# Sink keys and values of the later blocks folded into the preceding block's rows, with the displaced keys fetched in the load queue

## The chip, the cores and the metric

The kernel runs on one core of one Trainium2 chip. The metric is the device time of one execution in microseconds (us); a comparison uses runs of both kernels on the same chip, taken in the same rounds. Where runs of one kernel spread, those over 1.5% above its fastest count as slow, and ratios use the others.

## The reference, cut to what matters

Attention with four sink keys and a window of 128, per head, then a normalised MLP with a residual. Four batches, 8 heads, 768 rows, head size 64, so the row of the model has 512 elements.

```python
is_sink   = pos[None, :] < 4
rel       = pos[:, None] - pos[None, :]
in_window = (rel >= 0) & (rel < 128)
scores    = where(is_sink | in_window, scale * q @ k.T, -1e9)
a         = exp(scores - max) ; a = a / (sum(a) + 1e-9)
x         = concat_heads(a @ v)                        # (4, 768, 512)
xn        = (x - mean) / sqrt(var + 1e-6) * g_ln
out       = x + relu(xn @ w1) @ w2                     # 512 -> 2048 -> 512
```

The kernel cuts the rows into 24 blocks of 128, six to a batch. A block's queries see their own block, the block before (only those keys that the window reaches), and the four sinks of the batch. A block in row 2 to 5 of its batch sees the sinks in neither of those two blocks, so they need work of their own.

## The kernel before: the parts that matter

Every piece of work is a task with estimated costs per engine. A planner builds the static order of each engine's queue from them, and each engine works through its queue in that order. The planner takes, again and again, the ready task that can start first; what it believes about a cost decides what stands ahead of what. Blocks are taken in groups of four: a group's 4 x 128 rows go through the first MLP layer (`ph`, 64 wide matmuls) and the second (`pc`, 64 wide matmuls), and the attention of later blocks is laid between these matmuls.

```python
# scores of a block: window keys, then sinks (rows 2 to 5)
nc.tensor.matmul(ps[:, h2, hh, kb, :], lhsT=qkT[t - kb][rows, 1, hp, :], rhs=qkT[t][rows, 0, hp, :], ...)
for h2 in range(2):
    for hp in range(4):                                       # pk: 8 narrow matmuls
        nc.tensor.matmul(P["pk", t][32 * hp:32 * hp + 32, h2, :], lhsT=ks_of[b][:, h2, hp, :],
                         rhs=qkT[t][:, 0, hp, :], ...)
# ... cut: exponential on ScalarE, mask on VectorE ...
# values, per half block: two sink matmuls into po, then 8 window matmuls
nc.tensor.matmul(po[...][:, :, h2, :], lhsT=ES[t][:, h2, :], rhs=vs_t[b][...], ...)
nc.tensor.matmul(po[:, hh, :], lhsT=ee[:, h % 2, hh // 2, kb, :], rhs=vn[:, t - kb, h, :], ...)
# ... cut: normalisation po -> xt, sum -> xc (centred), then the transposed copy of xc ...

# loads, all in GpSimd's queue, in program order
def load(fn, land, take=(), desc=1024):
    i = plan.add({"POOL": 0.88}, [], fn, (0,), take=take, land=land, after=last_load[0], desc=desc)
# q and k of blocks 8 on, and all xc of later groups, are transposed by DMAs in SyncE's queue
DTR = set(range(8, NT))
```

Names used below: `qkn` is q and k of a block as loaded, `vn` its values, `qkT` the transposed q and k (scores need it), `xc` the centred rows, `xnt` their transposed copy (the first MLP layer needs all four blocks of a group), `ot` an output row. "SPq" and "POOLq" in a profile are the queues of SyncE and GpSimd. Groups are counted from 0 in tables, so group 2 is the third group; it holds blocks 8 to 11. "Landing" is the time from the issue of a DMA to its completion.

The softmax here doesn't subtract the row's maximum and nothing guards it: scores larger than these inputs give would overflow.

## Time and profile before

| | before |
|---|---|
| time | 227.5 us median (226.96 to 227.76) |
| TensorE busy | 217.0 of 225.4 us |
| first matmul of the first MLP layer | 20.26 us |
| scores of block 8 | 59.69 us |
| q of block 13 issued by GpSimd | 63.95 us |
| `xc` of block 11 written | 83.11 us |
| third group's first MLP matmul | 95.74 us |
| last matmul ends | 221.3 us |

The prediction below shows the page, the stages and the chain. Three lines of the timelines of before are added here. The columns are start (us), duration (us), engine, line, operation, output <- input, count, and in brackets the idle time ahead with what ended it.

```profile
59.69 0.62 PE L406 MATMUL ps<-qkT 64*128 64x128 bf16 x16 [0.45 <-DMA qkT<-qkn]
```

```profile
63.95 0.92 POOL L267 DMA_DIRECT2D qkn<-in_q_dram  x1
```

```profile
83.11 0.35 DVE L529 TENSOR_SCALAR xc<-xt,sums 128x512 bf16<-128x512 bf16 x1
```

TensorE waited only 0.45 us for block 8; block 13's q was under way 25 us before its scores (88.64 us).

### The profile page before, as it was taken

What the parts mean: (1) busy time and instruction counts of PE and PEld (TensorE: products, weight loads), DVE (VectorE), ACT (ScalarE), POOL (GpSimd) and SP (SyncE); (2) the same over time, 40 slices, a digit from 0 to 9 for tenths busy, and PEclk for the clock granted to TensorE, in tenths of its full rate; (3) what the DMA queues carried; (4) which work ended last, traced back from release to release, by engine and by line L of the source; (5) the groups of instructions that cost most, each with busy time, mean ns of one, the idle gap of its engine ahead of it and who ended that gap; (6) DMA issues with size and microseconds to landing.
All of it is one profiled execution on the core that took longest, in us unless ns stands there. A gap on an engine that the chain in (4) does not pass through costs nothing.

```text
span 225.4 us, 4783 instructions
## 1 busy us (share of the span) xinstructions
PE 217.0 (96%) x1921; PEld 121.0 (54%) x1948; DVE 135.0 (60%) x398; ACT 104.0 (46%) x166; POOL 76.0 (34%) x92
## 2 busy tenths in 40 slices
PE   8999999999999999999999999999999999999992
PEld 7766787655455554455555544454555544444440
DVE  5777998779577988863756873654854712100121
ACT  2386788344367731167641258633077600376000
POOL 7994366691695242933088000100000010000000
PEclk9999999999999999999999999999999999999999
DMA  7999999999999999999989994203221021200111
GB/s 43 139 157 206 182 184 209 166 173 192 218 150 129 144 140 189 175 185 191 94 103 158 168 209 88 51 17 102 71 48 23 3 70 47 93 0 3 47 71 69
DMA packets 108709, 26.52 MB, mean 118 GB/s; under 512 B 101520, under 2 KB 105616, under 8 KB 108688
## 3 DMA queue, kind: packets, MB, share of 16 engines
q0 software_dynamic: 79104, 13.64, 81.7%
q1 hardware_dynamic: 29584, 12.59, 30.1%
q8 instruction: 15, 0.25, 0.4%
q14 instruction: 6, 0.05, 0.1%
HBM read 27.27 MB, written 6.29 MB: 149 GB/s over the span
## 4 chain that ended last, share of the span: by engine, by line
PE 81%; DMA 8%; POOL 5%; DVE 3%; issue 1%; ACT 0%; POOLq 0%; ACTq 0%
PE ph L603 34%; PE pc L634 34%; PE ps L406 5%; DMA w1s<-in_moe_w_ch_dram 4%; DMA qkT<-qkn 3%; PE po L501 2%; PE po L504 2%; POOL qkn L267 2%; POOL vn L275 2%; POOL qkn L272 2%; PE po L496 2%; PE pk L413 1%; PE pt L347 1%; DVE xt L517 1%; DVE w1s L299 1%
## 5 line engine op out<-in xcount | busy, mean ns | idle before, releaser
L603 PE MATMUL ph<-xnt,w1s 128*128 128x512 bf16 (+1 forms) x434 | 88.9, 348 | 1.0 <-DVE h L617 0.3
L634 PE MATMUL pc<-w2s,h 128*128 128x512 bf16 x371 | 87.0, 379 | 1.1 <-issue 0.5
L619 ACT ACTIVATE h<-ph 128x512 bf16<-128x512 f32 (+1 forms) x84 | 45.8, 546 | 53.8 <-PE ph L603 52.1
L603 PEld LDWEIGHTS <-w1s 128*128 128x128 bf16 x448 | 41.5, 98 | 35.4 <-ACT h L619 0.5
L634 PEld LDWEIGHTS <-h 128*128 128x128 bf16 x384 | 35.8, 98 | 39.1
L435 ACT ACTIVATE e<-ps 128x1024 bf16<-128x1024 f32 (+1 forms) x48 | 43.7, 951 | 12.5 <-PE ps L406 12.5
L646 DVE SCALAR_TENSOR_TENSOR ot<-pc,rsg,xt 128x512 f32<-128x512 f32 x24 | 17.9, 747 | 38.9 <-PE pc L634 38.9
L548 POOL TENSOR_TENSOR rsg<-ve,eps_half 128x4 f32<-128x4 f32 x6 | 6.2, 1028 | 82.0 <-DVE ve L546 82.0
L267 POOL DMA_DIRECT2D qkn<-in_q_dram x24 | 21.9, 910 | 14.9 <-DMA qkT<-qkn 13.1
L444 DVE TENSOR_TENSOR e<-e,mask_std 128x1024 bf16<-128x1024 bf16 x28 | 18.9, 684 | 10.9 <-ACT e L435 10.9
L617 DVE TENSOR_SCALAR h<-ph 128x512 bf16<-128x512 f32 (+1 forms) x28 | 15.9, 570 | 13.7 <-PE ph L603 13.6
L272 POOL DMA_DIRECT2D qkn<-in_k_dram x24 | 21.7, 903 | 2.8 <-DMA w2s<-in_moe_w_ch_dram 1.4
L275 POOL DMA_DIRECT2D vn<-in_v_dram x24 | 21.8, 912 | 1.8 <-DMA w1s<-in_moe_w_ch_dram 1.8
L517 DVE SCALAR_TENSOR_TENSOR xt<-po,rc 128x256 bf16<-128x256 f32 x48 | 20.4, 425 | 1.7
L501 PE MATMUL po<-vn,e 128*128 128x65 bf16 x192 | 17.1, 193 | 0.1
L537 DVE BATCH_NORM_STATS2 st<-xt 128x6 f32<-128x512 bf16 x24 | 16.4, 684 | 0.0
L406 PEld LDWEIGHTS <-qkT 64*128 64x128 bf16 x352 | 9.9, 94 | 10.4 <-issue 7.8
L406 PE MATMUL ps<-qkT 64*128 64x128 bf16 x352 | 14.7, 218 | 0.7 <-DMA qkT<-qkn 0.4
L482 ACT ACTIVATE es<-pk 128x256 bf16<-128x256 f32 x16 | 6.1, 383 | 19.9 <-PE pk L413 19.8
L514 DVE RECIPROCAL rc<-po 128x4 f32<-128x4 f32 x48 | 8.5, 178 | 11.3 <-PE po L504 10.4
L501 PEld LDWEIGHTS <-e 128*128 128x128 bf16 x192 | 14.0, 97 | 2.1 <-DVE e L444 0.5
L504 PE MATMUL po<-vn,e 128*128 128x65 bf16 x160 | 14.9, 193 | 0.0
(66 smaller groups left out, 146.2 us busy)
## 6 DMA issues: line engine op xcount, KB each, us to landing
out_dram<-ot SPq DMA_DIRECT2D x24, 256.0 KB, 2.5
qkn<-in_q_dram POOLq DMA_DIRECT2D x24, 128.0 KB, 7.1
qkn<-in_k_dram POOLq DMA_DIRECT2D x24, 128.0 KB, 6.8
vn<-in_v_dram POOLq DMA_DIRECT2D x24, 128.0 KB, 7.6
w1s<-in_moe_w_ch_dram POOLq DMA_DIRECT2D x4, 512.0 KB, 10.3
w2s<-in_moe_w_ch_dram POOLq DMA_DIRECT2D x4, 512.0 KB, 10.7
qkT<-qkn SPq DMA_TRANSPOSE x16, 7.2
xnt<-xc SPq DMA_TRANSPOSE x16, 5.6
```

The lines of the kernel that those rows point to most:

```text
L267: nc.gpsimd.dma_start(qn[t][:, 0], q[b, :, rows, :].rearrange("h p d -> p h d"))
L272: nc.gpsimd.dma_start(qn[t][:, 1], k[b, :, rows, :].rearrange("h p d -> p h d"))
L275: nc.gpsimd.dma_start(vn[:, t, :, 0:64], v[b, :, rows, :].rearrange("h p d -> p h d"))
L406: nc.tensor.matmul(ps[:, h2, hh, kb, :], lhsT=qkT[t - kb][rows, 1, hp, :], rhs=qkT[t][rows, 0, hp, :], start=(hh == 0 and kb == 0 and t no ...
L435: nc.scalar.activation(E[t, half][:, :, :, 0:nkb, :], P["ps", t, half][:, :, :, 0:nkb, :], AF.Exp, scale=scale)
L444: nc.vector.tensor_mul(ee[:, :, 0:w], ee[:, :, 0:w], m[:, 0:w].unsqueeze(1).to_broadcast([128, 4, w]))
L501: nc.tensor.matmul(po[:, hh, :], lhsT=ee[:, h % 2, hh // 2, 0, :], rhs=vn[:, t, h, :], start=(r < 2 and hh == 0), stop=(r == 0), skip_grou ...
L504: nc.tensor.matmul(po[:, hh, :], lhsT=ee[:, h % 2, hh // 2, 1, :], rhs=vn[:, t - 1, h, :], start=False, stop=True, skip_group_check=True)
L517: nc.vector.scalar_tensor_tensor(xt[t][:, 256 * half:256 * half + 256].rearrange("p (h d) -> p h d", h=4), in0=po[:, :, 0:64], scalar=1.0, ...
L603: nc.tensor.matmul(ph, lhsT=w1s[:, j, 128 * ht:128 * (ht + 1)], rhs=xnt[g][:, j, cols], start=(j == 0), stop=(j == NDM - 1))
L619: nc.scalar.activation(o, i, AF.Relu)
L634: nc.tensor.matmul(P["pc", t], lhsT=h1[g, ht][:, 128 * ti:128 * (ti + 1)], rhs=w2s[:, ht, :], start=(ht == 0), stop=(ht == NH1 - 1))
```

## The change

The first four keys of the preceding block are almost useless to a later block: key 0 is outside the window of all its queries, and keys 1 to 3 are seen only by queries 0 to 2. So in blocks 14 to 17 and 20 to 23 the batch's sink keys and values are written over rows 0 to 3 of the preceding block's, after that block has used them. The window matmuls then do the sinks' work as well, and the eight sink matmuls for scores and four for values of each such block disappear. What queries 0 to 2 lose is computed apart: their rows of q, and the three displaced keys and values, are fetched in a row layout, worked out on VectorE in fp32 for all blocks at once ("the corrections"), spread by three DMAs (`fcb`), and added into `po` before the normalisation.

Besides, the planner gets other lags and start times for the opening, and may put a block's variance on ScalarE.

```diff
+    FOLD = 12
+    FETCH = 13
+        fold = r >= 2 and t >= FOLD
+            def fold_k(e): nc.vector.tensor_copy(qkT[t - 1][:, 1, :, 0:4], kss_of[b])
+            def fold_v(e): nc.vector.tensor_copy(vn[0:4, t - 1], vn[0:4, t - r])
-            sink = r >= 2 and halves[-1] == 1
+            sink = r >= 2 and not fold and halves[-1] == 1
...
+    def fetch(i, b):                              # row i of batch b: three small loads
+        def f(e):
+            nc.gpsimd.dma_start(fq[at], q[b, :, 256:768, :]...[i])
+            for to, src in ((fk, k), (fv, v)):
+                nc.gpsimd.dma_start(to[at]..., src[b, :, 129:641, :]...[:, :, 0:3, :]...)
+        fetched.append(load(f, .35, desc=96 * 3, cost=1.2))
...
+    def corrections():
+        def step(cost, deps, fn, eng="DVE"):
+            return plan.add({eng: cost}, deps, fn, (0, 7, 8))
+        # 3 products with q, 3 sums, exp, mask, 3 products with v, 1 sum, 2 additions
+        # then fcb[i:i + 1] <- fc[12 * i:12 * i + 12] for i in 0..2, on SyncE
...
+                if fold:
+                    nc.vector.tensor_add(po[0:3], po[0:3], fcb[:, t - RB - 2 * b, 4 * half:4 * half + 4, :])
...
+        if t == FETCH:                            # in the load queue ahead of block 13
+            for b in range(1, B):
+                for i in range(3):
+                    fetch(i, b)
         load_block(t)
```

(Cut: the new lags of loads and filler of the opening, the model of two DMA queues in the planner, smaller rings, and the ScalarE form of the variance.)

## The prediction

> **What bounds the kernel now.** I read the page first (busy shares, then the 40 slices), then the busy time by stages, the chain that ended last, and last the groups by shape.
>
> ```profile
> PE 217.0 (96%) x1921; PEld 121.0 (54%) x1948; DVE 135.0 (60%) x398; ACT 104.0 (46%) x166; POOL 76.0 (34%) x92
> ...
> PE   8999999999999999999999999999999999999992
> ```
>
> TensorE is busy 217.0 of 225.4 us; no other engine passes 60%. Only the first and the last slices fall off. By stages (us; busy time and count of PE, PEld, DVE, ACT, POOL; clock; DMA; GB/s):
>
> ```profile
> 20.00:26.50 6.50, 5.91 (x71) 4.51 (x69) 6.13 (x23) 5.13 (x11) 2.51 (x3) 1.00 1.40 199
> ...
> 60.50:79.10 18.60, 18.39 (x197) 10.13 (x198) 14.84 (x42) 13.85 (x22) 11.93 (x14) 1.00 2.03 157
> 79.10:95.80 16.70, 16.49 (x134) 8.41 (x135) 14.00 (x45) 3.86 (x5) 9.04 (x11) 1.00 1.77 168
> ...
> 179.80:221.30 41.50, 41.25 (x189) 18.58 (x190) 5.84 (x11) 10.15 (x17) 1.01 (x1) 1.00 0.14 48
> ```
>
> From 26.5 us on, TensorE is the bound in every stage. A microsecond of matmuls removed there is a microsecond off the end, unless a new wait appears. DVE has its least room from 79 to 96 us: 14.00 of 16.70 us. Up to about 20 us the loads set the time and TensorE is kept busy with filler matmuls. The chain that ended last, in order of time (start, us, what), shows what is to be removed:
>
> ```profile
> 105.20 0.62 PE ps L406 x16
> 105.82 0.23 PE pk L413 x8
> 106.05 2.70 PE ph L603 x12
> 108.74 0.12 PE po L496 x2
> ```
>
> Each block with a sink pays 0.23 us for eight narrow score matmuls (pk), and, for each half, 0.12 us for two sink matmuls into po. In the same chain 16 window-score matmuls take 0.55 us, and 49 wide ones 10.74 us, or 0.216 to 0.219 us each.
>
> [...] So the durations by group (220 to 380 ns) are latencies, and counts must be multiplied by steps. [...] q loads show 0.91 us on GpSimd and 7.1 us to landing. [...]
>
> **The change, part by part.**
>
> Removed on TensorE: eight blocks (14 to 17, 20 to 23) lose their sink matmuls, 8 x (0.23 + 2 x 0.12) = 3.8 us. Batches 2 and 3 lose two spreading matmuls each (pv), 4 x 0.11 = 0.44 us. **4.2 us**, all in the PE-bound part.
>
> Moved on TensorE: I compared the static order of the two builds. One half-block of attention (0.36) and one block's transposes (0.22) now stand ahead of the first MLP matmul, where the first w1 chunk (landing about 20 us) sets the time, and three filler matmuls after it are gone (0.15). That is 0.7 us more. Multiplying the two instruction lists from that matmul on by the steps above gives 196.0 us before and 191.1 after: **4.9 us**. In the trace the same stretch takes 201.0 us (20.3 to 221.3), so 5.0 us of small waits come on top, 1.5 of them before 26.5 us while DVE scales w1 between the last normalisations. I expect 0.3 of these to go, as the rescaled filler lets the early blocks finish sooner. Fillers ahead of 20 us cost nothing. The tail (last output row, store) is the same.
>
> DVE: added are 16 three-row additions in PSUM (0.41 each by the planner's own cost: 6.6 us), eight pairs of row copies (0.56 a pair: 4.5) and the corrections, 11 operations of 512 fp32 elements and four small ones, 11 x 0.69 + 0.8 = 8.4 us. Removed are four vs products (424 ns) and four ks copies (320), 3.0 us, and 13 of 24 variances (684 + 182 ns, 11.3 us), which go to ACT in the new order. With four more wide relus (0.69 each) the sum is about +8 us, 143 of 222. No bound on average. ACT gets 13 variances of about 1 us each (estimate from its 128x512 passes at 597 ns plus the small scaling) and loses eight exponentials (383 ns), four relus and a few copies: 104 to about 110. No bound.
>
> GpSimd and loads: 27 small loads enter the queue ahead of block 13. The one-core trace gives two sizes: 1024-descriptor loads start 0.87 apart, the four w1 loads of 512 descriptors (15.23 - 12.25)/4 = 0.745 apart. A straight line through these puts 32 descriptors at 0.62 us, so 27 take 16.9 us; the planner allows 0.4 each, 10.8 us.
>
> ```profile
> 58.56 1.03 POOL L548 TENSOR_TENSOR rsg<-ve,eps_half 128x4 f32<-128x4 f32 x1 [7.20 <-DVE ve L546]
> 59.56 0.93 POOL L272 DMA_DIRECT2D qkn<-in_k_dram  x1
> ...
> 84.39 0.74 DVE L646 SCALAR_TENSOR_TENSOR ot<-pc,rsg,xt 128x512 f32<-128x512 f32 x1
> 85.05 0.17 DVE L514 RECIPROCAL rc<-po 128x4 f32<-128x4 f32 x1
> ```
>
> Here GpSimd sits in order behind the power of group 1. In the new order that power follows block 3's output row, which ended just after 59.9 us; so the power ends near 62, block 12's k and v near 63.5, and the fetches start then. At 0.4 each they are issued by 74.3[...]; at 0.62 by 80.3[...]. The first correction stands in DVE's queue just after the first normalisation of block 11. In the new PE order block 11 comes earlier than the 85 us above: 54.8 us of work after the first MLP matmul, with 3.2 us of waits, or 78.3 on TensorE and 79.3 on DVE. **So at 0.4 us per fetch nothing waits, and at 0.62 DVE stands still about 3 us.** DVE is in order, so block 12's masks, block 11's centring and the output rows queue behind. TensorE has 44 wide matmuls (9.5 us) queued that need little of DVE, and the corrections take 8.4 us of that. A stall of 3 us on DVE therefore passes about 2 us on to TensorE, at block 12's AV near 91 or at the third group's first MLP matmul near 95. Block 13 itself, loaded at 80 to 82 in this case, transposed by 87 or 88, meets a need at 89.
>
> The row copies wait for the previous block's scores and AV, some 8 us earlier; I charge nothing.
>
> **The sum.** 4.9 + 0.3 = 5.2 us if the fetches are cheap, less about 0.3 for crowding on DVE: 227.5 - 4.9 = 222.6. At 0.62 us per fetch: 5.2 - 2.3 = 2.9, or 224.6. I weigh the first slightly more, for the planner's other costs (0.9 a load) match the trace: **223.3 us**.
>
> **Rivals.** (1) *The load queue becomes the wait.* If each fetch takes what a full load takes, 0.87 us, they end at 87,[...] DVE stops for 10 us and block 13 comes 5 us late: some 7 us lost, 229. For it: GpSimd's time depends little on the count of descriptors (0.745 against 0.87 for half). Against: it does depend. (2) *DVE becomes the bound around 79 to 96 us.* It had 14.0 of 16.7 us there; 8.4 us of corrections do not fit unless the variances leave it (they do, four or five of them, 4 us) and some work moves later. Block 11's centring is delayed behind them, and its transposed copy is needed by the third group. That alone would cost 1 to 3 us: 223.5 to 225.5. (3) *The removed work is all there is,* and earlier progress is lost again, because block 8's transposed q and k set the time at 59.7 us (TensorE waited 0.45 us there): then only 4.2 us, 223.3. (4) *The opening gains more than I charge:* all 1.5 us of waits before 26.5 go: 221.5.
>
> **Range and chances.** The 2% line is 222.94 us. Cheap fetches and an orderly DVE fall just below it, everything else above. I give 45% to fetches near 0.4 us (mostly below the line), 40% to some 0.6 (mostly above), 15% to dearer ones. That makes 0.41 for faster, 0.56 for within 2%, and 0.03 for slower, which would take 232 us. Range 221.0 to 226.8.
>
> **What would show it right or wrong.** In the profile after: pk 64 and po<-vs 32 instead of 128 and 64, PE busy down by 4 to 5 us. The spacing of the fetches on GpSimd is the number to look for: 0.4 or 0.6. The first correction's product on DVE should show idle time released by a DMA only in the latter case, and TensorE then a gap between 88 and 97 us. From 110 to 180 us each half of a group should be shorter by what the sinks cost, with TensorE at 98% as before. I am wrong if the gap on TensorE comes without a wait for the fetches (DVE crowding, or the transposes), if the additions to po hold PSUM banks so long that the stages after 110 us do not shorten, or if the start of the first MLP matmul moves from 20.3 us.

Cut from it, where marked, are rules that no trace of this case shows, and the landing time of a small load that was taken from one of them. The forecast of 223.3 us, between 222.6 (0.4 us a fetch) and 224.6 (0.62), was summed with that landing time, so terms of it are cut: it is a part of the 3 us for which VectorE was to stand still, of the 2.3 us taken off for them, and of the 10 us of rival (1). The numbers that stay have the fetches issued by 74.3 or 80.3 us against a first correction at 79.3; the rest of the 3 us was an assumption that no trace had shown. The steps by which the counts are multiplied can be read from the chain of before: 0.216 to 0.219 us for a wide matmul, 0.06 us for one into `po` of 130 columns (two in 0.12 us at 108.74), 0.055 us for one of 128 columns (four transposes in 0.22 us at 45.26). For the 0.69 us of a 512-element fp32 operation on VectorE that trace has only near ones: the statistics pass at 684 ns, the relu at 685 ns.

## The result, and the profile after

The changed kernel takes **238.31 us** (median of four runs, 236.60 to 239.85) against 227.52 us (226.96 to 227.76). The ratio is 1.0476, 95% interval 1.0388 to 1.0564: slower. A ratio here is the mean time of one kernel's fast runs over the mean of the other's of the same rounds, so it is not quite the ratio of the medians. Predicted were 223.3 us and a range to 226.8.

The page of after: busy times, TensorE in 40 slices, and the granted clock in the same slices (before, every slice of the clock was 9). The granted clock is the share of TensorE's full clock that the profile records.

```profile
PE 215.3 (92%) x1813; PEld 118.7 (51%) x1836; DVE 142.1 (61%) x420; ACT 109.6 (47%) x190; POOL 92.2 (39%) x120
...
PE   8799999999799994496999999999999999999993
...
PEclk9999999999999999587999999999999999999999
```

A slice is 5.87 us. The loss lies in three of the four slices from 88 to 111 us (4, 4, 9, 6); the clock is down in the last three of these (5, 8, 7). By stage, after and then before (same columns as in the prediction):

```profile
79.10:95.80 16.70, 11.37 (x76) 5.50 (x74) 10.77 (x25) 2.63 (x6) 16.61 (x23) 0.97 1.15 91
95.80:112.00 16.20, 11.92 (x85) 5.98 (x87) 8.57 (x31) 7.36 (x14) 7.71 (x9) 0.71 1.99 171
```

```profile
95.80:112.00 16.20, 15.95 (x147) 8.31 (x149) 9.46 (x26) 10.40 (x16) 3.73 (x5) 1.00 1.96 164
```

TensorE fell from 16.49 and 15.95 us to 11.37 and 11.92 us of work, and in the second stage that work ran at a mean clock of 0.71. GpSimd, by contrast, has not a free moment from 79 to 96 us: 16.61 of 16.70. VectorE is *less* busy than before, 10.77 against 14.00: it is not overloaded, it waits.

When the stages begin shows where the 9.6 us come from by which the last matmul of the profiled run ends later (start of each layer's first matmul, us):

| | before | after | difference |
|---|---|---|---|
| layer 1, group 1 | 60.47 | 61.19 | +0.72 |
| layer 2, group 1 | 79.09 | 80.17 | +1.08 |
| layer 1, group 2 | 95.74 | 107.57 | +11.83 |
| layer 2, group 2 | 112.75 | 125.28 | +12.53 |
| layer 2, group 3 | 145.63 | 157.03 | +11.40 |
| layer 2, group 4 | 179.66 | 189.23 | +9.57 |
| last matmul ends | 221.26 | 230.84 | +9.58 |

From 125 us on the changed kernel *regains* 3.0 us, which is the folding at work. Some 10.75 us are lost in one stage. The waits of TensorE around it:

```profile
60.41 0.62 PE L484 MATMUL ps<-qkT 64*128 64x128 bf16 x16 [1.76 <-DMA qkT<-qkn]
...
97.08 1.03 PE L484 MATMUL ps<-qkT 64*128 64x128 bf16 x16 [6.45 <-DMA qkT<-qkn]
...
107.57 1.02 PE L714 MATMUL ph<-xnt,w1s 128*128 128x512 bf16 x4 [2.15 <-DMA xnt<-xc]
```

Block 13's scores wait 6.45 us for its transposed q and k; ten microseconds later the third group's MLP waits for block 11's transposed copy. The chain that ended last (start, us, what; the pieces over these 60 us) runs through the second of these, not the first:

```profile
51.06 9.31 DMA qkT<-qkn
60.90 0.88 POOL qkn L295
...
63.71 8.84 DMA vn<-in_v_dram
73.42 5.02 DMA fv<-in_v_dram
84.56 2.28 DMA fv<-in_v_dram
98.63 8.81 DMA xnt<-xc
107.57 1.02 PE ph L714 x4
```

Each step can be seen in the queue of its engine. GpSimd first:

```profile
64.58 0.64 POOL L365 DMA_DIRECT2D fq<-in_q_dram  x1
...
70.84 0.59 POOL L365 DMA_DIRECT2D fq<-in_q_dram  x1 [2.71 <-DMA qkn<-in_k_dram]
72.84 0.59 POOL L367 DMA_DIRECT2D fk<-in_k_dram  x1 [1.41 <-DMA vn<-in_v_dram]
...
84.56 0.59 POOL L367 DMA_DIRECT2D fv<-in_v_dram  x1
85.14 0.95 POOL L295 DMA_DIRECT2D qkn<-in_q_dram  x1
```

The fetches start 0.58 to 0.61 us apart: 27 of them take some 15.8 us. Besides, three of them wait, 4.8 us in all, for a load issued earlier to land; each time it is the load eight places before in this queue (the seventh fetch waits for block 12's k, with block 12's v and six fetches between). Block 12's k and v took 7.8 and 8.8 us to land and so hold the fetch up. The instructions in the trace show where the eight comes from: the loads of this queue use eight completion semaphores in turn (numbers 99 to 106), and a load first waits on the one that it is to use (96 of the 99 loads after the first eight), that is for the landing of the load that had it last. So this wait is built into the program (kernel.py itself names no semaphore), and one slow load stops the queue eight loads later. Block 13's q is issued at 85.14, 21.2 us later than before. Then VectorE:

```profile
80.94 0.15 DVE L376 TENSOR_SCALAR mask_c<-iota_c 36x3 f32<-36x3 int32 x1
86.82 0.68 DVE L383 TENSOR_TENSOR fk<-fk,fq 36x512 f32<-36x512 f32 x1 [5.72 <-DMA fv<-in_v_dram]
...
96.17 0.35 DVE L634 TENSOR_SCALAR xc<-xt,sums 128x512 bf16<-128x512 bf16 x1
```

The planner believed in 0.4 us a fetch and placed the corrections where they would then have been ready. VectorE stands 5.72 us at the first of them, and block 11's `xc` comes behind the last, at 96.17 instead of 83.11. (The name in brackets is the profile's guess. The product waits for all eight semaphores; the last one to be reached was that of the last k fetch, issued at 83.98 and landed at 86.79. The last fetch of all, of v, issued at 84.56, landed at 87.72.) Last SyncE's queue:

```profile
96.03 2.49 SPq L397 DMA_DIRECT2D fcb<-fc  x3
98.63 1.42 SPq L676 DMA_TRANSPOSE xnt<-xc  x1
```

The three DMAs of the corrections go out just ahead of block 11's transposing DMA, which then takes 8.81 us to land, while the loads of blocks 13 on are being caught up. Which of the two makes that landing long is not separated by any run.

So there are **two ways** from the late fetch to TensorE: (a) block 13's own loads, (b) VectorE's wait, the corrections, block 11's `xc` and its transposed copy. The first hypothesis on this trace was that (a) with the lowered clock behind it is the loss; the chain favours (b). The experiments decide.

### The profile page after: what moved, and what is told of

Same layout as the page of the kernel before. It is cut to its first block, busy times and chain, and to the rows that moved or that the text cites. A ratio compares the mean times of both kernels' runs of the same rounds, so it can differ in the third digit from the quotient of the medians.

```text
span 234.8 us, 4652 instructions
## 1 busy us (share of the span) xinstructions
PE 215.3 (92%) x1813; PEld 118.7 (51%) x1836; DVE 142.1 (61%) x420; ACT 109.6 (47%) x190; POOL 92.2 (39%) x120
## 4 chain that ended last, share of the span: by engine, by line
PE 69%; DMA 16%; POOL 5%; DVE 5%; issue 2%; ACT 1%; SPq 1%; POOLq 0%; DVEq 0%
PE ph L714 30%; PE pc L745 27%; DMA qkT<-qkn 4%; PE ps L484 4%; DMA vn<-in_v_dram 4%; DMA xnt<-xc 4%; DMA fv<-in_v_dram 3%; DMA qkn<-in_q_dram 2%; PE po L601 2%; PE po L604 1%; PE pt L425 1%; POOL fk L367 1%; PE ps L475 1%; DVE ot L757 1%; DVE fk L383 1%
## 5 line engine op out<-in xcount | busy, mean ns | idle before, releaser
L730 ACT ACTIVATE h<-ph 128x512 bf16<-128x512 f32 (+1 forms) x79 | 43.0, 546 | 42.9 <-PE ph L714 42.3
L745 PEld LDWEIGHTS <-h 128*128 128x128 bf16 x384 | 36.3, 99 | 41.1 <-issue 1.8
L728 DVE TENSOR_SCALAR h<-ph 128x512 bf16<-128x512 f32 (+1 forms) x33 | 19.0, 581 | 12.5 <-PE ph L714 12.4
L484 PE MATMUL ps<-qkT 64*128 64x128 bf16 x352 | 15.5, 226 | 8.2 <-DMA qkT<-qkn 8.2
L484 PEld LDWEIGHTS <-qkT 64*128 64x128 bf16 x352 | 10.5, 98 | 17.9 <-DMA qkT<-qkn 8.9
L533 DVE TENSOR_TENSOR e<-e,mask_one 128x1024 bf16<-128x1024 bf16 x22 | 14.6, 686 | 4.4 <-ACT e L524 4.4
L601 PEld LDWEIGHTS <-e 128*128 128x128 bf16 x192 | 14.2, 99 | 4.5 <-DVE e L533 0.6
L604 PEld LDWEIGHTS <-e 128*128 128x128 bf16 x160 | 11.1, 97 | 2.2
L648 ACT ACTIVATE nb<-sums 128x1 f32<-128x1 f32 x13 | 2.6, 201 | 17.6 <-DVE sums L631 17.6
## 6 DMA issues: line engine op xcount, KB each, us to landing
w2s<-in_moe_w_ch_dram POOLq DMA_DIRECT2D x4, 512.0 KB, 10.9
```

The lines of the kernel that those rows point to most:

```text
L601: nc.tensor.matmul(po[:, hh, :], lhsT=ee[:, h % 2, hh // 2, 0, :], rhs=vn[:, t, h, :], start=(not sinks and hh == 0), stop=(r == 0), skip_ ...
L604: nc.tensor.matmul(po[:, hh, :], lhsT=ee[:, h % 2, hh // 2, 1, :], rhs=vn[:, t - 1, h, :], start=False, stop=True, skip_group_check=True)
L730: nc.scalar.activation(o, i, AF.Relu)
L745: nc.tensor.matmul(P["pc", t], lhsT=h1[g, ht][:, 128 * ti:128 * (ti + 1)], rhs=w2s[:, ht, :], start=(ht == 0), stop=(ht == NH1 - 1))
```

## The experiments

In every case the edit is on the changed kernel unless another is named. The kernel before took 227.5 to 228.0 us (medians). Runs named "wrong on purpose" leave up to three query rows of eight blocks uncorrected; that stays within the tolerance of the comparison.

### Take away the fetch, the corrections, or both

```diff
 # no fetch (wrong on purpose): three memsets on GpSimd in place of the 27 loads
-            nc.gpsimd.dma_start(fq[at], ...)       # and fk, fv
+            if (i, b) == (0, 1): nc.gpsimd.memset(fq, 0.0); nc.gpsimd.memset(fk, 0.0); nc.gpsimd.memset(fv, 0.0)
 # no corrections (wrong on purpose): planned as before, nothing emitted; zeros added into po
-            return plan.add({eng: cost}, deps, fn, (0, 7, 8))
+            return plan.add({eng: cost}, deps, lambda e: None, (0, 7, 8))
```

> The changed kernel with the 27 fetches of displaced rows not issued; three memsets on GpSimd stand in for them, so the corrections run on zeros (wrong result on purpose), everything else in the same order. Theory A (the fetches in the load queue make block 13's load and DVE's corrections late): the idle time of 6.5 us before block 13's scores, the wait of 5.7 us on DVE and the lower clock from 96 to 112 us all go; about 224 us. Rival B (the 8 us of corrections crowd DVE whatever the fetch does): 229 to 233, with TensorE still waiting for block 11's transposed copy. Rival C (the folding itself, or the planner's other changes): 234 or more.

> The changed kernel with all 27 fetches, but without the corrections on DVE and ACT and without the spreading DMAs; the additions to po add zeros (result wrong in the first three rows of eight blocks on purpose). Theory A in its first half (the load of block 13 comes late because it stands behind the fetches): TensorE still idles some 5 to 6 us before block 13's scores and the clock still falls; 231 to 235 us. Theory A in its second half (DVE waits for the fetch, and all that stands behind it is late) or rival B: the time falls to 224 to 227. Rival C: no change, 237.

> The changed kernel without fetches and without corrections (wrong result on purpose in the first three rows of eight blocks): the folding of the sinks alone, in the same order of instructions. Theory A and rival B: about 223 to 224 us, since 3.8 + 0.44 us of matmuls are gone from the bound stages and block 8 sets the time at 60 us as before. Rival C in its first half (folding brings its own waits): 230 or more.

| | median us | ratio to before | 95% interval |
|---|---|---|---|
| fetch and corrections (the change) | 238.31 | 1.0476 | 1.0388 to 1.0564 |
| corrections alone (no fetch; one run of four slow) | 229.35 | 1.0026 | 0.9961 to 1.0092 |
| fetch alone (no corrections) | 235.92 | 1.0328 | 1.0277 to 1.0378 |
| neither (one run of four slow) | 225.16 | 0.9866 | 0.9829 to 0.9902 |

Without either, the folding is worth 1.3%: the saving of the prediction is real, though smaller than predicted. The fetch in its place costs most (10.8 us without corrections), the corrections without it 4.2 by the medians. Not all of the 4.2 is theirs: in the profiled executions the run without the fetch is 6.0 us behind the one with neither at the last matmul, and 3.0 of these it had lost by 82 us, ahead of the first correction, where block 8's scores waited 2.00 us instead of 0.99 and the clock behind it was lower (0.64 from 60.6 to 62 us, 0.50 to 64, 0.90 to 66). TensorE's waits, first without the fetch, then without the corrections:

```profile
101.23 1.18 PE L713 MATMUL ph<-xnt,w1s 128*128 128x512 bf16 x4 [2.75 <-DMA xnt<-xc]
```

```profile
98.42 1.04 PE L483 MATMUL ps<-qkT 64*128 64x128 bf16 x16 [7.10 <-DMA qkT<-qkn]
```

Each takes one way away and leaves the other: without the fetch block 13 is in time and only `xnt` is late; without the corrections `xnt` is in time and block 13 is as late as ever. Taking (b) away wins only 2.4 us of the 13, because (a) then sets the time. The lowered clock is on the path in that run: it was 0.50 from 94.3 to 104.6 us, so after the wait of 7.10 us the 6.1 us from 98.4 on lose (1 - 0.50) x 6.1 = 3.1 us more, 10.2 of the 10.8 together (an estimate).

### The planner's other changes alone

```diff
-    FOLD = 12
+    FOLD = 99          # no block folds; no fetch, no corrections
```

> The changed kernel with no block folded, no fetches, no corrections: only the planner's other changes (costs, filler, variance on ACT, smaller rings) over the kernel before; correct result. Theory A: 226.5 to 228.5 us, neutral. Rival C in its second half (the other changes cost the time): 232 or more. If the other changes had given something, 225 or less.

229.81 us, ratio 1.0051 (1.0001 to 1.0101; one run of four slow). The rest of the change is worth nothing or a little less than nothing. Block 8's scores waited 2.54 us in its profiled execution, the slow one. The waits at block 8 return below.

### Keep TensorE's clock up: filler matmuls in the wait

```diff
+                    if t == 13 and half == halves[0]:
+                        for _ in range(110):                # 6.3 us ahead of block 13's scores
+                            nc.tensor.matmul(ps..., lhsT=ident, rhs=ident, ...)
```

> The changed kernel with 110 filler matmuls (some 6 us) put ahead of block 13's scores, where TensorE stood idle 6.5 us. If the lower clock after that idle time costs by itself (in the trace 1.5 us at 0.50, 6.1 us at 0.74 and 4.5 us at 0.62, some 4 us of work lost), the clock stays up to block 13's successors and the time falls by 2 to 4 us, to 233 to 235. If only the idle time counts, no change or slightly slower: 237 to 239.

239.75 us, ratio 1.0504 (1.0437 to 1.0571): no gain, although the mean clock from 95.8 to 112 us rose from 0.71 to 0.92.

```profile
98.82 0.62 PE L488 MATMUL ps<-qkT 64*128 64x128 bf16 x16 [1.72 <-DMA qkT<-qkn]
...
109.96 1.87 PE L718 MATMUL ph<-xnt,w1s 128*128 128x512 bf16 x4 [4.99 <-DMA xnt<-xc]
```

What the clock gave back before 105 us was spent waiting for `xnt`. So the low clock between 97.1 and 101.7 us was *not on the path* of the change; (b) was. (The comparison is not exact: in this execution VectorE waited 6.60 us for the fetch instead of 5.72, and block 11's `xc` came 1.2 us later.) My expectation of the clock as part of the loss was wrong.

### A smaller fetch: batches 2 and 3 only

```diff
-            for b in range(1, B):        # 27 loads, corrections on 36 rows
+            for b in range(2, B):        # 18 loads, corrections on 24 rows
```

> The changed kernel with fetches and corrections for batches 2 and 3 only: no block of batch 1 is folded, so nine of the 27 fetches are never used. Correct result. 9 x 0.585 = 5.3 us less in the load queue. Theory A: the idle time before block 13's scores falls from 6.5 to about 1.2 us, DVE's wait from 5.7 to about 0.4, and the clock dips less: 228 to 231 us. If the loss came from the corrections on DVE instead (unchanged here, 36 or 24 partitions take the same time): 235 or more.

234.38 us, ratio 1.0298 (1.0253 to 1.0342).

```profile
92.38 0.62 PE L484 MATMUL ps<-qkT 64*128 64x128 bf16 x16 [0.54 <-DMA qkT<-qkn]
...
105.65 1.87 PE L714 MATMUL ph<-xnt,w1s 128*128 128x512 bf16 x4 [5.27 <-DMA xnt<-xc]
```

Way (a) is open here (0.54 us) and the time is still 3% above before: way (b) alone. VectorE waited 3.67 us for the fetch, and here that also reached TensorE directly: at 88.84 it waited 2.17 us for a mask that stands behind the first corrections. The 512-element operations of the corrections took 0.67 to 0.68 us on 24 rows here, as on 36 rows in the change. I had expected 228 to 231, having seen only (a).

### Leave all the work and tell the planner what it costs

```diff
-        fetched.append(load(f, .35, desc=96 * 3, cost=1.2))    # three loads
+        fetched.append(load(f, .35, desc=96 * 3, cost=2.1))
```

> The changed kernel with the planner told 2.1 us for each set of three fetches instead of 1.2 (the trace has 20.6 us for the 27, with waits), so that the static order fits. Theory: most of the loss came from an order that was planned with a wrong cost; MLP matmuls of the third group move ahead of block 13 and the corrections behind work that is ready: 226 to 230 us, DVE's wait for the fetch under 1 us. Rival: the load queue itself is late and every later block with it, whatever the order: 233 or more.

229.35 us, ratio 1.0037 (0.9972 to 1.0101; one run slow). The same 27 loads and corrections, ordered for 0.7 us a load, give back some 9 us. The wait was not gone, as I had expected (under 1 us): in the profiled execution VectorE still stood 4.25 us for the fetch, whose loads waited 7.1 us for others instead of 4.8. The profiled execution (231.82 us, the slow one) still had three waits on TensorE:

```profile
61.92 0.62 PE L484 MATMUL ps<-qkT 64*128 64x128 bf16 x16 [2.33 <-DMA qkT<-qkn]
...
95.33 5.30 PE L745 MATMUL pc<-w2s,h 128*128 128x512 bf16 x16 [2.08 <-DVE ot L757]
...
102.64 0.56 PE L484 MATMUL ps<-qkT 64*128 64x128 bf16 x14 [2.01 <-DMA qkT<-qkn]
```

### The smaller fetch with the corrections placed later

Edit: the fetch of batches 2 and 3, and priority (0, 13, 8) for the corrections instead of (0, 7, 8). Block 11's `xc` and its transposing DMA then stand ahead of most corrections and of `fcb`.

> The fetch of batches 2 and 3 alone (18 small loads in GpSimd's queue), with the corrections placed later in DVE's order, so that most of them and their three DMAs come after block 11's centring and its transposing DMA. Theory of two gates (block 13's late load, and DVE and SyncE held up ahead of block 11's centring and its transposed copy): both are open, waits at block 13 below 1 us and at the third group's first MLP matmul below 1.5 us, that matmul at 96 to 98.5 us, and a time of 227 to 230. Rival (late loads by themselves slow whatever follows: the transposing DMA lands late because the loads catch up): that matmul still waits 3 us or more, and the time is 232 to 235.

232.75 us (229.49 to 234.14; two of four runs count as slow, so no ratio). The wait for `xnt` is gone: the third group's MLP begins at 100.84 without one. But block 13 waits 2.08 us, and the normalisations behind late `fcb` hold TensorE 1.81 us near 116. In the profiled execution (232.5) the idle time between 26.5 and 146 us adds up to 6.4 us, and the lowered clock (0.91 over 60 to 79 us, 0.95 over 112 to 146) to some 3.4 more, (1 - 0.91) x 18.6 + (1 - 0.95) x 33.8, an estimate. The third-group half of the expectation held, the time did not.

### Fetch through SyncE's queue, early, and corrections late

```diff
-            nc.gpsimd.dma_start(fq[at], ...)                  # 27 loads, GpSimd
+            nc.sync.dma_start(fq[at], q[2:4, :, ...]...)      # 9 loads, SyncE, rows (batch, head)
+        # gated by a tiny memset on VectorE behind the last w1 load, so that they start near 30 us
-            return plan.add({eng: cost}, deps, fn, (0, 7, 8))
+            return plan.add({eng: cost}, deps, fn, (0, 13, 8))
```

> Folding as in the change, but the displaced rows of batches 2 and 3 are laid out by (row, batch, head), which takes nine DMAs; these go on the SyncE queue, which is idle between 3 and 46 us, after the w1 loads; the corrections have half the columns (256) and a low priority. Correct result. Theory A: no wait for the fetches and none for block 13: 223.5 to 225.5 us, as without fetch and corrections. If the corrections still crowd DVE or the small DMAs hold up the loads: 227 or more.

227.64 us, ratio 0.9985 (0.9944 to 1.0026), results correct. TensorE worked 16.70 of 16.70 us from 79.1 to 95.8 and 16.20 of 16.20 from 95.8 to 112, at a clock of 1.00: both ways are open, with nothing of the fold or its corrections given up. The edit changes the queue, the number of loads, their time, the width of the corrections and their place all at once, so it does not say which of these was needed. I had expected 223.5 to 225.5 us; what was left stood earlier, in this wait and this stage:

```profile
62.51 0.62 PE L486 MATMUL ps<-qkT 64*128 64x128 bf16 x16 [2.49 <-DMA qkT<-qkn]
```

```profile
60.50:79.10 18.60, 16.08 (x173) 8.60 (x174) 12.58 (x34) 11.19 (x18) 11.58 (x13) 0.91 2.05 160
```

### On top of it, block 8 (and 9) transposed on TensorE, and the old opening

```diff
-        elif t in DTR:
+        elif t in DTR and t > 8:       # block 8's q and k: matmuls with the identity, not a DMA
```

> The nine loads by SyncE and the late corrections, and block 8's q and k transposed on TensorE instead of by a DMA. Theory (what kept that arrangement level with the kernel before is the wait of 2.49 us for block 8's transposed q and k and the clock of 0.91 granted over the 18 us after it): the wait goes, 60.5 to 79.1 us show a clock of at least 0.97, the extra transposes cost about 0.3 us, and the time is 223.5 to 225.5. Rival (the loads themselves come too late there, whoever transposes): a wait of 1.5 us or more stays ahead of block 8's scores or transposes, and the time is 226.5 or more.

225.55 us (223.19 to 226.53), ratio 0.9900 (0.9859 to 0.9942). The same stage:

```profile
60.50:79.10 18.60, 18.04 (x204) 9.74 (x202) 15.96 (x47) 12.19 (x20) 8.92 (x10) 1.00 2.17 133
```

The wait and the clock of 0.91 are gone, and with them 2 us. The largest wait after 26.5 us is 0.71.

The next run also puts the planner's opening back to that of the kernel before (lags, start times, filler):

> As the run with block 8 on TensorE, and the opening (lags of loads, cost of the first filler, filler pace, start times) as the planner of the kernel before has it. Theory (block 8's wait alone): as that run within 1 us, 223.5 to 226. Rival (the change's new opening costs time by itself, as the first MLP matmul went from 20.26 to 22.05 us): the first MLP matmul is back near 20.3 and the time is 1 us or more below that run's.

225.16 us (222.84 to 225.86), ratio 0.9877 (0.9838 to 0.9917). The first MLP matmul came at 20.96 instead of 23.08 us, but the two intervals overlap: 2.1 us at the start of the MLP are not 2.1 us at the end. In the version that starts it later more of the other work has been done by then.

The last takes block 9 from the DMAs too:

> As the run with SyncE's nine loads, block 8 on TensorE and the old opening, and block 9 on TensorE as well. Theory (the 1.14 us that TensorE waited for block 9's transposed copies set the end): that wait goes and the time falls by 0.4 to 1 us, to 224.2 to 224.8. Rival (something else ends the time there, as DVE's masks near 85 us): the time stays within 0.4 us of 225.2, and a wait of the same size shows later.

224.87 us (224.32 to 226.62), ratio 0.9894 (0.9858 to 0.9930). The wait of 1.14 us at block 9 is gone; the time has not moved beyond the intervals. These three are the correct versions that beat both kernels, the one before by 1.0 to 1.2%; none reaches 2%.

### Move the fetch into GpSimd's idle time

In the trace after, GpSimd stood idle for 8.18 us just ahead of block 12's loads (the 51.06 and 60.90 lines of the chain), and the fetch came after. Was the place the cause?

```diff
-    FETCH = 13
+    FETCH = 11
```

> The change with one number altered: the fetch stands in the load queue ahead of block 11's loads instead of block 13's, same 27 loads, same corrections. In the trace of the change GpSimd was idle for 8.2 us between the loads of block 11 and block 12. Theory (the place is the cause: the fetch came after that idle stretch instead of filling it): the first 18 small loads start near 50 us and fill the idle stretch, the fetch is over by 68, block 13's q is issued by 75 instead of 85, waits at block 13 and at the third group's first MLP matmul fall below 1.5 us each, and the time is 227 to 231. Rival (27 small loads of 0.59 us and the corrections are too much wherever they stand): another block, 11 or 12, is late by 3 us or more or DVE waits 3 us or more, and the time is 233 or more.

> As the run with the fetch ahead of block 11, and block 8's q and k transposed on TensorE. Theory (place of the fetch plus block 8's wait are all that was lost): no wait on TensorE over 1.5 us after 26.5 us, and 224 to 227. Rival (the fetch in the load queue costs something by itself, as the corrections crowd DVE ahead of the third group): 228 or more, with waits over 1.5 us left between 79 and 112 us.

240.97 us, ratio 1.0538 (1.0485 to 1.0591), and with block 8 on TensorE 237.49 us, ratio 1.0401 (1.0366 to 1.0435): **the theory of the place fell**. The fetch did start at 50.30 us, but it took until 75.3, because the loads of eight places before landed slowly (8.0 us of waits), and the planner, with its 0.4 us, moved the corrections forward with it. VectorE, then TensorE, of the first run:

```profile
78.79 0.68 DVE L383 TENSOR_TENSOR fk<-fk,fq 36x512 f32<-36x512 f32 x1 [6.17 <-DMA qkn<-in_q_dram]
```

```profile
81.44 7.39 PE L714 MATMUL ph<-xnt,w1s 128*128 128x512 bf16 x24 [6.31 <-DVE h L728]
```

The wait followed the belief, not the place: the next section sets the belief right at this same place, and 1.0401 becomes 1.0155. (The wait at 78.79 is put down to a block's load in the same queue; the last fetch was issued at 74.67.)

### The true cost, with block 8 on TensorE, at both places

Edit: `cost=2.1` as above, `t > 8` as above, `FETCH` 13 and then 11.

> The change with the planned cost of three fetch loads set to 2.1 us instead of 1.2, and block 8's q and k transposed on TensorE; fetch still at block 13. Theory (the same 27 loads and corrections cost little once the order is made for their real time, and block 8's wait was the largest one left): 226 to 228, no wait over 1.2 us between 60 and 79 us. Rival (waits move to the next place, as the pc and ps waits of 2 us near 95 and 103 us in the run with the true cost alone): 229 or more, with those waits kept or grown.

> As the run before, with the fetch ahead of block 11. Theory (place costs nothing once the corrections stand where the fetch has landed): no DVE wait for the fetch over 1.5 us, and a time within 2 us of the run before, 225 to 229. Rival (at this place the loads in flight ahead hold the fetch up, as it took 25 us there, and blocks 11 and 12 come late): 231 or more with a wait for block 11's or 12's transposed q and k.

At block 13: 233.71 us, but from 226.69 to 236.88; five of six runs count as slow, so there is no ratio, and the run is inconclusive. At block 11: 233.00 us (229.87 to 235.35), ratio of the fast half 1.0155 (1.0111 to 1.0198). Neither expectation held. The profiled executions are slow ones and only illustrate: at block 13 the fetch took from 61.80 to 88.04 us, with 10.9 us of waits for loads to land, against 4.8 in the change and 5.0 at block 11, and VectorE waited 6.47 us. The issue of a fetch is steady at 0.59 us in all of them; the waits between are not. In these runs a fetch in this queue has no one true cost, and neither of the two planned costs tried (0.4 and 0.7 us) made its order safe. Why the landings vary so from one arrangement, and one execution, to the next is left open.

## Why the prediction was wrong

**"Removed on TensorE ... 4.2 us".** Right in kind, and mostly in size. From 125 us on the changed kernel regains 3.0 us, where six of the eight folded blocks pay 0.47 us each, or 2.8. With neither fetch nor corrections the time falls by 1.3%, or 3.1 us. Predicted were 5.2 in all. Where the other 2 us went is not isolated; the profiled execution shows the first MLP matmul 1.17 us later than before (21.43), 0.99 us of wait at block 8 instead of 0.45, 0.52 for the third group's transposed copy, and 0.56 for the row copies ahead of block 14's scores, to which the prediction charged nothing.

**"A straight line through these puts 32 descriptors at 0.62 us".** Right: 0.58 to 0.61. The step that failed is the sum after it, which has the fetches issued "at 0.62 by 80.3". It left out that a load in this queue may have to wait for the load eight places before to land. That cost 4.8 us here, so the last fetch was issued at 84.56 and landed at 87.72. The landing of small rows, for which I used a value that no trace had shown, was 2.8 us at the least and had medians of 3.8 to 4.8.

**"DVE stands still about 3 us".** It stood 5.72, for the same reason. (The line at 85.05 that the prediction reads as block 11's normalisation is block 12's; block 11's first was at 80.58. That did no harm: the sum used 79.3, and 80.37 was measured.)

**"A stall of 3 us on DVE therefore passes about 2 us on to TensorE ... Block 13 itself, loaded at 80 to 82 in this case, transposed by 87 or 88, meets a need at 89."** This is the step that cost the range. I treated the two consequences of a late fetch as one small stall and one near miss. Block 13's q was issued at 85.14, its scores waited 6.45 us. And the stall on VectorE was not absorbed by queued matmuls: it lay on the chain of `xc`, `fcb` in SyncE's queue and `xnt`, with a landing of 8.81 us at its end. The prediction set 8.4 us of corrections against 9.5 us of queued matmuls and left that landing out; before, the copy had landed only 5.7 us ahead of its use, and now its `xc` came 13.1 us later. These run side by side: opening one alone won 2.4 us (no corrections) or 3.9 us (the smaller fetch), removing the causes of both 13.2. That both are the loss is shown by these runs; the SyncE version, which changes more at once, agrees. That the order planned for 0.4 us a fetch is at fault is shown by the true-cost run, where only that number differs; its remaining waits differ, so it doesn't isolate each wait.

**Rival (1), "the load queue becomes the wait"**, 229 us, was the right one, and I gave it 15%. I made it depend on a fetch costing 0.87 us. It came at 0.59, by the waits between the fetches; and I gave it only one way to TensorE.

**Rival (2), VectorE as the bound at 79 to 96 us**, was half right. With the corrections but without the fetch VectorE was busy 15.47 of 16.70 us there, and `xnt` waited 2.75 us; the run was 4.2 us slower than with neither. In the profiled executions about 3.0 us of the difference lie behind the first correction, the upper end of the 1 to 3 us that I gave it.

**Rival (3), progress lost again at block 8**, held and was mis-sized: 1.76 us of wait in the change and 2.0 to 2.5 in several runs, instead of 0.45. Taking block 8 from the DMAs won 2 us once the larger waits were gone (227.64 to 225.55). **Rival (4), gains in the opening**, did not show: the first MLP matmul moved from 20.26 to 22.05 us, and restoring the old opening changed nothing measurable.

**Costs on VectorE and ScalarE** were right: 36x512 fp32 products took 672 to 684 ns against 0.69 us predicted, additions to `po` 420 ns against 0.41, the ScalarE variances 0.72 + 0.20 + 0.19 us against "about 1 us". DVE came to 142.1 us against 143 predicted. Busy times were not where this prediction failed.

**The test "PE busy down by 4 to 5 us"** is a weak one: it fell only from 217.0 to 215.3, because matmuls at a lowered clock count as longer (the sixteen score matmuls of block 13 took 1.03 us behind the wait, those of block 8 0.62). With neither fetch nor corrections it was 211.9, 5.1 down.

**What the clock did.** In the traces of before and after the record of the granted clock holds only 1.00 and 0.50; figures between, as 0.71, are means over a stage. Before, it was 1.00 in every stage from 20 us to the last matmul. In the change it was 0.50 from 94.9 to 101.7 us (6.8 us), around the end of the 6.45 us wait, and from 108.6 to 112.0 us (3.4 us), behind the wait for `xnt`. The prediction left this out. The first stretch was hidden (filler experiment); the second lies on the path: (1 - 0.50) x 3.4 = 1.7 us, an estimate, in keeping with the 0.70 us lost in that layer net of the fold, which takes 0.47 us from each of two blocks there.

## What to carry to other kernels

When a change puts many small transfers into a queue that also feeds the main work, count issue times (27 x 0.585 us here), then the waits for earlier transfers to land (4.8 us here), and then follow *every* consumer behind them to its need; two consumers late by the same cause hide each other, so an experiment that cures one shows little, and the chain that ended last names only the longer. An order that a planner builds on a cost below the real one turns a cheap addition into stalls of in-order engines: here the same work was 9 us faster when only the planned cost was corrected, though not reliably so beside other edits; and with the transfers early in a queue with room and their use late, TensorE did not wait for them at all.

## What was measured of the load queue and the clock

- A small load of 32 contiguous runs (8 or 24 KB) kept GpSimd 0.58 to 0.61 us in the changed kernel, against 0.87 from start to start for a load of 1024 runs (128 KB by the DMA table).
- Small loads took 2.8 us at the least to land, and 3.8 to 4.8 us by the medians, in the changed kernel (DMA table), and medians of up to 7.9 us in the run with the true cost and block 8 on TensorE.
- In these programs a load in GpSimd's queue can have to wait for the load eight places before it to land. These waits took 4.8 us of the fetch in the changed kernel, 8.0 and 10.9 us in two other runs. The limit is the program's: the trace shows eight completion semaphores used in turn. What the chip itself would allow, the runs do not show.
- One transposing DMA, for `xnt` of block 11, took 8.81 us to land while the loads were being caught up; the median of the 16 of `xnt` in that trace is 5.0 us.
- The clock was 0.50 around the end of the wait of 6.45 us, and lower after some shorter waits too: after 1.81 us (the late corrections; 0.95 on average from 112 to 146 us), 2.00 us (no fetch; 0.91 from 60.5 to 79.1) and 2.49 us (the SyncE run; 0.91 from 60.5 to 79.1). After others of that length it stayed at 1.00: 1.98 us (no corrections) and 2.33 us (the true cost), both 1.00 from 60.5 to 79.1, and 2.17 us (the smaller fetch), 1.00 from 79.1 to 95.8. So in these runs the length of a wait alone does not tell what the clock does.
